# A static scheduler with other durations, VectorE/GpSimd access in its plan, paced attention, and two thirds of batch 0 masked by multiplication

## The chip, the cores and the metric

The kernel runs on one core of a Trainium2 chip, in one launch. The metric is the device time of one execution in microseconds (us). Five engines work beside each other, each through its own queue in order: TensorE (PE in the profile: matmuls; its weight loads are PEld), VectorE (DVE), ScalarE (ACT), GpSimd (POOL) and SyncE (SP, which only issues transfers here).

## The reference

Block-sparse attention (4 batches, 8 heads, 768 positions, head width 64), then a two-layer network with a squared relu on the 3072 x 512 result.

```python
scores = scale * np.matmul(q, k.transpose(0, 1, 3, 2))
mask = np.abs(blk_i - blk_j) <= window          # blocks of 32, window 1
mask = mask | (blk_i == 0) | (blk_j == 0) | (blk_i == n_blocks - 1) | (blk_j == n_blocks - 1)
for qb in range(n_blocks):
    for kb in sampled_blocks[qb]:               # 3 drawn blocks per query block
        mask[qb * block:(qb + 1) * block, kb * block:(kb + 1) * block] = True
scores = np.where(mask, scores, -1000000000.0)
attn = softmax(scores)
x = matmul(attn, v) as 3072 x 512
out = (np.maximum(x @ w_in, 0.0) ** 2) @ w_out  # 512 -> 2048 -> 512
```

## The kernel before

**Pairs and slots.** Two heads of one batch form a pair, 16 in all, 0 to 3 being batch 0. Work on attention is cut into 144 slots, each of one pair, 256 query columns (`qi`, 0 to 2) and 256 keys (`cp`, 0 to 2). Batch 0 goes by query third, then pair, then keys: slots 0 to 11 are `qi` 0 of its four pairs. From slot 36 on a pair's nine slots follow each other.

**A slot.** `scores` (L323) makes eight groups of 64-row matmuls, two heads side by side, into one of two PSUM buffers `ps`. `exps` (L341) is one exponential of 128 x 1024 on ScalarE into `pT`. `values` (L355) multiplies `pT` by the values, eight 65-wide matmuls into `po`; the 65th column gives the row sum. After three slots `normalize` (VectorE), `x_transp` (TensorE) and `x_evac` write 256 columns of `xT`.

**The mask** comes in two ways. In batch 0 `scores` adds it: four more matmuls on L337 of the block mask `R2` by `oh`. In the other batches `masks` (L346) multiplies `pT` on VectorE by `MK`, a 0/1 mask in SBUF that `mask_tile` and `mask_evac` (L258, L265) make in six tiles of 768 columns.

**Making a pair ready** (`prepare`, L459). For batch 0 queries and keys are cast to bfloat16 (`cast_qk`), transposed on TensorE (`transp`) and copied out (`evac`, into `QK`); from pair 4 on a DMA transposes (`transp_dma`, on SP's queue). Loads of pairs 4 and on wait at `loads_gate` until named parts of the network's weights have landed. `w_load` (L304) issues the weights in eight parts on GpSimd's queue, after the values of pair 2 were cast.

**Dense part.** `hidden`, `relu`, `square`, `output`, `out_copy`, `store`, over tiles of 256 tokens (batch 0) and 384 tokens. A relu goes to VectorE or ScalarE, a square to GpSimd, ScalarE or VectorE.

**Who orders all this.** Each step is a `Task` with engines and durations in us (`T_({"DVE": 0.57, "POOL": 1.0}, key, ...)`), the tasks it depends on, buffers it takes and gives back. `run_schedule` (L96) runs a plan when the program is built: of all ready tasks it takes the one with the earliest start, then the smallest key, puts it on the engine that would end first (plus a `bias`), and emits its instructions. Its durations set only the order in each engine's queue; at run time the engines wait on semaphores alone.

Of the kernel before, what the change touches and what calls it, by code (L numbers as in the profile page):

```python
# [25 lines left out]
def kernel(  # L26
# [32 lines left out]
    NRAW, NPB = 4, 6  # L59
# [17 lines left out]
    LAT = {"PE": 0.2, "DVE": 0.08, "ACT": 0.08, "POOL": 0.08, "SP": 2.0}  # L77
    SWITCH = 0.15
# [5 lines left out]
    class Task:  # L84
        def __init__(self, engs, key, fn, deps=(), get=(), put=(), after=0.0, mode=None, dma=0.0, late=None, bias={}):
# [3 lines left out]
            self.after, self.mode, self.dma, self.late, self.bias = after, mode, dma, late, bias  # L89
            self.end = self.eng = None  # L90
            self.order = len(tasks)
            for b in self.put:
                b.holds += 1
            tasks.append(self)

    def run_schedule(free, bufs, dma_free, mode=128):  # L96
        taken = {name: [] for name in bufs}
        waiting = list(tasks)
# [6 lines left out]
        while waiting or ready:  # L105
# [5 lines left out]
            best = None  # L111
            for t in ready:
# [26 lines left out]
            t.end = free[e] = end  # L139
# [42 lines left out]
    load(3, (sc_, sy, sc_))  # L182
# [39 lines left out]
    sbf = consts.tile([nb, n_rand], F32, name="sbf")  # L222
    edge = consts.tile([nb, 2], F32, name="edge")
    pm = consts.tile([nb, 4, nb], F32, name="pm")
    V.tensor_scalar(out=pm[:, 0, :], in0=rel, scalar1=-1.0, scalar2=None, op0=AOP.is_ge)
    V.scalar_tensor_tensor(out=pm[:, 1, :], in0=rel, scalar=1.0, in1=pm[:, 0, :],
                           op0=AOP.is_le, op1=AOP.mult)
    V.tensor_scalar(out=edge[:, 0:1], in0=row, scalar1=0.0, scalar2=None, op0=AOP.is_equal)
    V.tensor_scalar(out=edge[:, 1:2], in0=row, scalar1=float(nb - 1), scalar2=None, op0=AOP.is_equal)
    V.tensor_scalar(out=pm[:, 0, :], in0=pm[:, 1, :], scalar1=edge[:, 0:1], scalar2=edge[:, 1:2],  # L230
                    op0=AOP.max, op1=AOP.max)
    V.memset(pm[:, 0, 0:1], 1.0)
    V.memset(pm[:, 0, nb - 1:nb], 1.0)
    V.tensor_copy(out=oh[D:P, :], in_=oh[0:D, :])
    V.tensor_copy(out=sbf, in_=sb_i.rearrange("q (r two) -> q r two", two=2)[:, :, 0])
    cur = 0
    for r in range(n_rand):
        V.scalar_tensor_tensor(out=pm[:, 1 - cur, :], in0=col, scalar=sbf[:, r:r + 1],
                               in1=pm[:, cur, :], op0=AOP.is_equal, op1=AOP.max)
        cur = 1 - cur  # L240
    for c0 in (0, D):
        V.tensor_scalar(out=bm[:, c0:c0 + nb], in0=pm[:, cur, :], scalar1=-1.0, scalar2=-NEG,
                        op0=AOP.add, op1=AOP.mult)
# [5 lines left out]
    pb = ps_s.tile([P, 1024], F32, name="pb", tag="ps")  # L249
    for j, c0 in enumerate((0, 512)):  # L250
        w = min(512, S - c0)
        nc.tensor.matmul(pb[:, c0:c0 + w], bm, oh[0:nb, c0:c0 + w], start=True, stop=True)
    A.copy(out=R2[:, 0:QW], in_=pb[:, 0:QW])
    A.copy(out=R2[:, QW:S], in_=pb[:, QW:S])
# [3 lines left out]
    def mask_tile(n, e):  # L258
        pk = ps_s.tile([P, 1024], F32, name="pk", tag="ps")
        for c0 in (0, 512):  # L260
            w = min(512, S - c0)
            nc.tensor.matmul(pk[:, c0:c0 + w], oh[:, n * P:(n + 1) * P], R2[:, c0:c0 + w], start=True, stop=True)
        mtile[n] = pk

    def mask_evac(n, e):  # L265
        pk = mtile.pop(n)
        if e == "ACT":
            A.activation(out=MK[:, n, :], in_=pk[:, 0:S], func=AF.Exp)  # L268
        else:
            V.tensor_scalar(out=MK[:, n, :], in0=pk[:, 0:S], scalar1=-1.0, scalar2=None, op0=AOP.is_ge)  # L270
# [13 lines left out]
    def transp(u, w, e):  # L284
        src = cast.pop((u, w))
        pt = ps_h.tile([P, S], BF, name="pt", tag="h")
        for n in range(NCH):
            nc.tensor.transpose(pt[:, n * P:(n + 1) * P], src[:, n].rearrange("p t d -> p (t d)"), identb)
        ttile[u, w] = pt

    def evac(u, w, e):
        copy(e, QK[u % NPB][:, w, :], ttile.pop((u, w)))

    def transp_dma(u, w, e):
        sy.dma_start(out=QK[u % NPB][:, w, :].rearrange("r (n p) -> r n p", p=P),
                     in_=cast.pop((u, w)).rearrange("p n t d -> p (n t d)"), transpose=True)

    w_in_sb = consts.tile([P, KM, d_ff], BF, name="w_in_sb")
# [5 lines left out]
    def w_load(i, e):  # L304
        if i < NWP:
# [143 lines left out]
    def arrive(u, w):  # L449
        return 5.7 + 1.6 * (3 * u + w)  # L450
# [8 lines left out]
    def prepare(u):  # L459
        s0 = first[u]  # L460
        tr[u], ev[u] = [], []
# [3 lines left out]
        if u >= HP:  # L465
            g = gate[2] if u == HP else gate[5] if u == HP + 1 else gate[7]
            ld_t = T_(("SP", 1.0), s0 - 30, load, u, (sy, sy, sy),
                      deps=cv[u - NRAW] + tr[u - NRAW] + [g], dma=4.3)
            at = dict(deps=[ld_t])
            for w in (1, 0):  # L470
                qc = Buf("qc")
                c = T_({"DVE": 0.57, "POOL": 1.0}, s0 - 12, cast_qk, u, w, get=[qc], **at)
                tr[u].append(c)
                ev[u].append(T_(("SP", 1.0), s0 - 10, transp_dma, u, w, deps=[c] + old_s, put=[qc], dma=1.2))
        else:
            at = dict(after=arrive(u, 2))
            for w in (0, 1):
                qc, hb = Buf("qc"), Buf("h")
                opts = {"ACT": 0.75} if u == 0 and w else {"DVE": 0.57}
                c = T_(opts, s0 - 6, cast_qk, u, w, after=arrive(u, w), get=[qc])  # L480
                tr[u].append(c)
                t = T_(("PE", 0.36), s0 - 5, transp, u, w, deps=[c], get=[hb], put=[qc], mode=128)
                ev[u].append(T_({"DVE": 0.57} if w else {"ACT": 0.75, "DVE": 0.57}, s0 - 4, evac, u, w, deps=[t], put=[hb]))
        cv[u] = [T_({"POOL": 1.0} if u in (1, 2) else {"POOL": 1.0, "DVE": 0.57}, s0 - 2, cast_v, u,
                    deps=at.get("deps", []) + old_v, after=at.get("after", 0.0))]
# [6 lines left out]
    def attend(group, add):  # L492
        s = min(order.index(a) for a in group)
        bufs = {a: Buf("ps") for a in group}
        u0 = [a[0] for a in group]
        sc = T_(("PE", (0.44 if add else 0.22) * len(group)), s, scores, group, add,
                deps=sum((ev[u] for u in u0), []) + sc_all[-1:], get=[bufs[a] for a in group], mode=64)
        sc_all.append(sc)
        for a in group:
# [9 lines left out]
            va = T_(("PE", 0.40), s + 2.2, values, a, deps=[ex] + cv[u] + va_all[-1:],  # L509
# [3 lines left out]
            if cp == CP - 1:  # L513
                b, a_ = divmod(u, HP)
                nm = T_(("DVE", 0.55), s - 9, normalize, u, qi, deps=[va])
# [5 lines left out]
                mu[u, qi] = T_({"DVE": 0.25, "ACT": 0.36}, s - 9, x_evac, u, qi, deps=[xt], put=[ob[u, qi]], **kw)  # L521

    sc_all, va_all, ob = [], [], {}
    for u in range(NU):
        sc_of[u], va_of[u] = [], []
    for us in [range(HP)] + [[u] for u in range(HP, NU)]:
# [17 lines left out]
    RELU = {256: {"DVE": 0.35, "ACT": 0.42}, 384: {"DVE": 0.48, "ACT": 0.50}}  # L544
    SQ = {256: {"POOL": 0.65, "ACT": 0.42, "DVE": 0.35}, 384: {"POOL": 0.82, "ACT": 0.50, "DVE": 0.48}}
    sq_of, n_key = {}, 1000.0
    gbuf, hbuf = {}, {}
    for k_, T in enumerate(TILES + [None]):
# [4 lines left out]
        for _, kind, x in sorted(both, key=lambda z: z[:2]):  # L553
# [3 lines left out]
            if kind == 0:  # L557
# [11 lines left out]
                sq_of[x] = T_(SQ[w], n_key, square, t, f, deps=[rr], get=[gb], put=[rb], bias={"ACT": 1.5, "DVE": 1.5})  # L569
            else:  # L570
# [47 lines left out]
```

## Time and profile before

| what | value |
|---|---|
| median of three runs | 309.04 us (308.96 to 312.02) |
| the profiled execution: time, span | 309.11 us, 307.4 us |
| TensorE, VectorE, ScalarE, GpSimd busy | 93%, 66%, 56%, 50% of the span |
| exponentials (L343) | 144, mean 1026 ns, from 12.58 us to 224.5 us |
| mask multiplications (L350) | 108, mean 822 ns |
| mask matmuls in batch 0 (L337) | 144 |
| squares on GpSimd (L421) | 144 |
| relus on VectorE, on ScalarE (L412, L410) | 112, 32 |

Rows of the view by stage give a stretch in us, its length, then per engine the busy time and the number of instructions in it, at the end the granted share of TensorE's clock, the share of the DMA engines and GB/s. Rows by form give line, engine, operation, output and inputs, shapes, count, busy us and mean ns, then the engine's idle time before these and who ended it. Timeline rows begin with start and duration in us.

### The profile page before, as it was taken

To read this page: it belongs to the slowest core of one execution; us is meant where nothing else is said; L and a number is where in the kernel's file an instruction comes from. 1 tells how busy PE (TensorE), PEld (TensorE's weight loads), DVE (VectorE), ACT (ScalarE), POOL (GpSimd) and SP (SyncE) were. 2 spreads that over 40 slices of the span, in tenths; PEclk is the share of its full clock that TensorE was granted. 3 is DMA by queue.
4 is the path that set the end of the run, shared out by engine and by line. 5 is a ranking of instruction groups with operands and counts; after the bars stand their busy time and mean duration, and the time that the engine had idled before them with its cause. 6 is when DMAs were issued, how large, how long until landed. Compare 5 with 4: busy or idle time off the path is not lost.

```text
span 307.4 us, 7318 instructions
## 1 busy us (share of the span) xinstructions
PE 284.8 (93%) x3002; PEld 166.2 (54%) x3002; DVE 203.1 (66%) x411; ACT 172.0 (56%) x217; POOL 152.6 (50%) x187
## 2 busy tenths in 40 slices
PE   6798999899898989889989999999989999999994
PEld 2456766675655544555546556455545555555542
DVE  7573334989998887889987787878774444444410
ACT  1878989107777877777878779788721000000011
POOL 4280111798756560466673344244436665666620
PEclk9999999999999999999999999999999999999999
DMA  7999998697999981320200000000100111000012
GB/s 259 355 138 205 260 256 304 175 280 205 255 232 247 256 199 48 74 53 2 51 2 36 3 34 2 36 35 2 36 0 36 41 50 49 35 34 36 34 47 89
DMA packets 40011, 34.55 MB, mean 112 GB/s; under 512 B 20522, under 2 KB 36906, under 8 KB 39978
## 3 DMA queue, kind: packets, MB, share of 16 engines
q1 hardware_dynamic: 34122, 27.53, 31.2%
q0 software_dynamic: 4224, 4.19, 8.5%
q10 hardware_dynamic: 1632, 2.36, 2.2%
q8 instruction: 23, 0.38, 0.5%
q14 instruction: 10, 0.08, 0.1%
HBM read 27.26 MB, written 6.29 MB: 109 GB/s over the span
## 4 chain that ended last, share of the span: by engine, by line
PE 59%; DVE 19%; ACT 10%; issue 5%; DMA 3%; POOL 2%; SPq 0%; ACTq 0%; DVEq 0%; POOLq 0%
PE ph L403 21%; PE py L433 20%; DVE pT L350 10%; PE po L366 7%; ACT pT L343 7%; PE ps L333 7%; DVE r L412 3%; DVE qc L158 2%; DVE xq L375 2%; POOL g L421 2%; DMA qs<-in_q_dram 2%; PE po L382 2%; PE ps L337 2%; DMA vs<-in_v_dram 1%; ACT MK L268 1%
## 5 line engine op out<-in xcount | busy, mean ns | idle before, releaser
L421 POOL TENSOR_TENSOR g<-r 128x384 bf16<-128x384 f32 (+1 forms) x144 | 125.0, 877 | 119.4 <-DVE r L412 96.0
L343 ACT ACTIVATE pT<-ps 128x1024 bf16<-128x1024 f32 x144 | 140.0, 1026 | 36.9 <-PE ps L333 32.4
L403 PE MATMUL ph<-xT,w_in_sb 128*128 128x384 bf16 (+1 forms) x576 | 108.7, 309 | 0.4 <-DVE r L412 0.3
L433 PE MATMUL py<-w_out_sb,g 128*128 128x512 bf16 x384 | 104.2, 379 | 0.1
L350 DVE TENSOR_TENSOR pT<-pT,MK 128x1024 bf16<-128x1024 bf16 x108 | 87.2, 822 | 6.5 <-ACT pT L343 6.4
L412 DVE TENSOR_SCALAR r<-ph 128x384 f32<-128x384 f32 (+1 forms) x112 | 57.1, 513 | 42.1 <-POOL g L421 24.0
L403 PEld LDWEIGHTS <-w_in_sb 128*128 128x128 bf16 x576 | 51.1, 98 | 36.7 <-issue 6.9
L366 PE MATMUL po<-VT,pT 128*128 128x65 bf16 x1152 | 54.0, 194 | 8.2 <-DVE pT L350 6.3
L366 PEld LDWEIGHTS <-pT 128*128 128x128 bf16 x1152 | 44.1, 98 | 30.5 <-DVE pT L350 15.4
L156 ACT COPY ys<-py 128x512 f32<-128x512 f32 x21 | 12.3, 587 | 77.2 <-PE py L433 77.1
L333 PE MATMUL ps<-QK 64*128 64x256 bf16 x576 | 52.1, 272 | 1.8 <-ACT pT L343 0.8
L433 PEld LDWEIGHTS <-g 128*128 128x128 bf16 x384 | 35.3, 98 | 25.9 <-issue 2.1
L333 PEld LDWEIGHTS <-QK 64*128 64x128 bf16 x576 | 24.2, 94 | 18.4 <-issue 11.6
L373 DVE RECIPROCAL rs<-po 128x4 f32<-128x4 f32 x48 | 8.6, 179 | 29.8 <-PE po L366 29.7
L375 DVE TENSOR_TENSOR xq<-po,rs 128x256 bf16<-128x256 f32 x48 | 20.4, 424 | 1.7
L410 ACT ACTIVATE r<-ph 128x384 f32<-128x384 f32 (+1 forms) x32 | 14.5, 454 | 8.0 <-PE ph L403 7.5
L337 PE MATMUL ps<-R,oh 64*128 64x256 bf16 x144 | 17.7, 269 | 0.0
L382 PE MATMUL po<-identb,xq 128*128 128x128 bf16 x96 | 13.5, 222 | 3.9 <-DVE xq L375 3.6
L158 POOL CAST VT<-vs 128x768 bf16<-128x768 f32 x8 | 7.0, 883 | 20.1 <-PE po L366 12.1
L382 PEld LDWEIGHTS <-xq 128*128 128x128 bf16 x96 | 6.7, 97 | 16.0 <-DVE xq L375 11.6
L158 DVE COPY xT<-po 128x256 bf16<-128x256 bf16 x36 | 10.2, 284 | 2.5 <-PE po L382 2.5
L158 DVE CAST qc<-qs 128x768 bf16<-128x768 f32 x11 | 7.7, 700 | 0.0
(50 smaller groups left out, 83.7 us busy)
## 6 DMA issues: line engine op xcount, KB each, us to landing
out_dram<-ys SPq DMA_DIRECT2D x24, 256.0 KB, 2.0
qs<-in_q_dram SPq DMA_DIRECT2D x14, 384.0 KB, 4.7
vs<-in_v_dram SPq DMA_DIRECT2D x14, 384.0 KB, 6.5
ks<-in_k_dram SPq DMA_DIRECT2D x14, 384.0 KB, 4.9
w_in_sb<-in_moe_w_in_dram POOLq DMA_DIRECT2D x4, 512.0 KB, 7.9
w_out_sb<-in_moe_w_out_dram POOLq DMA_DIRECT2D x4, 512.0 KB, 19.9
ks<-in_k_dram ACTq DMA_DIRECT2D x2, 384.0 KB, 6.0
qs<-in_q_dram ACTq DMA_DIRECT2D x2, 384.0 KB, 5.2
```

The lines of the kernel that those rows point to most:

```text
L158: (V if e == "DVE" else G).tensor_copy(out=out, in_=in_)
L333: nc.tensor.matmul(ps[:, h, c, :], QK[i][hs, 1, ksl], QK[i][hs, 0, qsl], start=c == 0, stop=not add, skip_group_check=True)
L337: nc.tensor.matmul(ps[:, h, c, :], oh[hs, ksl], R2[hs, qsl], start=False, stop=True, skip_group_check=True)
L343: A.activation(out=pT, in_=stile.pop(a), func=AF.Exp, scale=scale)
L350: V.tensor_tensor(out=pT, in0=pT, in1=m[:, None].broadcast_to([P, 2, 2, QW]), op=AOP.mult)
L366: nc.tensor.matmul(po[:, qc, h, :], pT[:, h, c, qc * P:(qc + 1) * P], VT[i][:, h, n, 0:VW], start=(n == 0 and qc == 0 and h == 0), stop=n ...
L375: V.tensor_tensor(out=xq, in0=po[:, :, :, 0:D], in1=rs.broadcast_to([P, 2, 2, D]), op=AOP.mult)
L382: nc.tensor.transpose(pt[:, qc * P:(qc + 1) * P], xq[:, qc].rearrange("p h d -> p (h d)"), identb)
L403: nc.tensor.matmul(ph, w_in_sb[:, kc, f * P:(f + 1) * P], xT[b][:, kc, c0:c0 + w], start=(kc == 0), stop=(kc == KM - 1))
L412: V.tensor_scalar(out=r, in0=src, scalar1=0.0, scalar2=None, op0=AOP.max)
L421: (G if e == "POOL" else V).tensor_mul(out=g, in0=r, in1=r)
L433: nc.tensor.matmul(py, gtile[T, f][:, ts * P:(ts + 1) * P], w_out_sb[:, f, :], start=(f == 0), stop=(f == NF - 1))
```

## The change

The scheduler's tables get other durations and latencies, with a part of each task (`OVER`) that overlaps the next one on its engine. Tasks marked `port` are lengthened in the plan where VectorE and GpSimd work at once. Tasks with keys from 100 up may not be put ahead of an urgent one on their engine (`AHEAD`). Scores from slot 36 on are planned no earlier than 40 + 1.7 us per slot. In batch 0 only slots 0 to 11 add the mask by matmul; slots 12 to 35 go in twos and are multiplied on VectorE. The mask tiles are cut into 512 and 256 columns, in the buffers `h`. Pair 0 is cast, transposed and copied in two parts. A load of values moves from ScalarE's queue to SP's; the weight loads move ahead, behind a small copy (`held`) that waits for the keys of pair 2. Squares may no longer go to VectorE, and go to ScalarE with a smaller bias. The mask's preparation on small tiles is written with fewer instructions, and the copy of `oh` moves to ScalarE.

```diff
-    NRAW, NPB = 4, 6
+    NRAW, NPB, QC_BUFS = 4, 6, 5
...
-    LAT = {"PE": 0.2, "DVE": 0.08, "ACT": 0.08, "POOL": 0.08, "SP": 2.0}
-    SWITCH = 0.15
+    LAT = {"PE": 0.23, "DVE": 0.06, "ACT": 0.06, "POOL": 0.08, "SP": 2.0}
+    OVER = {"PE": 0.0, "DVE": 0.08, "ACT": 0.09, "POOL": 0.03, "SP": 0.0}
+    SWITCH = 0.1
+    AHEAD = {"PE": 0.05, "DVE": 0.2, "ACT": 0.25, "POOL": 0.0, "SP": 0.0}
+    LEAD = 12.0
+    PACE0, PACE, SINGLE, MASK_AT = 40.0, 1.7, 1, 12.0
...
+                    if e == "POOL" or (e == "DVE" and t.port):
+                        p0, p1 = port["DVE" if e == "POOL" else "POOL"]
+                        us += 0.7 * max(0.0, min(r + us, p1) - max(r, p0))
...
+            best = min((c for c in found if c[1] < 100 or c[0] + AHEAD[c[4][2]] < urgent.get(c[4][2], 1e9)),
+                       key=lambda c: c[:3], default=None)
...
-            t.end = free[e] = end
+            t.end, free[e] = end, end - OVER[e]
...
-    load(3, (sc_, sy, sc_))
+    load(3, (sc_, sy, sy))
...
-    V.tensor_copy(out=oh[D:P, :], in_=oh[0:D, :])
+    A.copy(out=oh[D:P, :], in_=oh[0:D, :])
...
     def w_load(i, e):
+        if i == 0:
+            G.tensor_copy(out=held, in_=raw[2][1][0:1, 0, 0, 0:2])
...
-                c = T_({"DVE": 0.57, "POOL": 1.0}, s0 - 12, cast_qk, u, w, get=[qc], **at)
+                c = T_({"DVE": 0.55, "POOL": 1.2}, 101, cast_qk, u, w, slice(0, NCH), bias={"POOL": 0.5}, get=[qc], port=True,
+                       after=PACE0 + PACE * (s0 - HP * NQ * CP) - LEAD, **at)
...
+            for ns in (slice(0, 2), slice(2, NCH)) if u == 0 else (slice(0, NCH),):
...
-                wl[i] = T_(("POOL", 1.2), s0 - 3 + i, w_load, i, deps=cv[HP - 2], late=2.0, dma=3.6)
+                wl[i] = T_(("POOL", 0.85), -50 + i, w_load, i, after=12.6, late=2.2, dma=2.65)
...
         sc = T_(("PE", (0.44 if add else 0.22) * len(group)), s, scores, group, add,
-                deps=sum((ev[u] for u in u0), []) + sc_all[-1:], get=[bufs[a] for a in group], mode=64)
+                deps=[ev[u][w, 2 if n else 0] for u, qi, cp in group for w, n in ((0, qi), (1, cp))]
+                + (mr[:1 + (group[0][1] > 0)] if add else []) + sc_all[-1:], get=[bufs[a] for a in group], mode=64,
+                after=PACE0 + PACE * (s - HP * NQ * CP) if s >= HP * NQ * CP else 0.0)
...
-            ex = T_(("ACT", 0.95), s, exps, a, deps=[sc], get=[pt], put=[bufs[a]])
+            ex = T_(("ACT", 1.02), s, exps, a, deps=[sc], get=[pt], put=[bufs[a]])
             if not add:
-                ex = T_(("DVE", 0.6), s - 1, masks, a, deps=[ex, mk[cp * 2], mk[cp * 2 + 1]])
+                ex = T_(("DVE", 0.68), s - 1, masks, a, deps=[ex, mk[cp * 2, qi], mk[cp * 2 + 1, qi]], port=True)
...
-            for a in mine:
+            singles = [a for a in mine if a[1] < SINGLE]
+            for a in singles:
                 attend([a], True)
+            mine = [a for a in mine if a not in singles]
+            for i in range(0, len(mine) - 1, 2):
+                attend(mine[i:i + 2], False)
...
-    RELU = {256: {"DVE": 0.35, "ACT": 0.42}, 384: {"DVE": 0.48, "ACT": 0.50}}
-    SQ = {256: {"POOL": 0.65, "ACT": 0.42, "DVE": 0.35}, 384: {"POOL": 0.82, "ACT": 0.50, "DVE": 0.48}}
+    RELU = {256: {"DVE": 0.424, "ACT": 0.39}, 384: {"DVE": 0.557, "ACT": 0.49}}
+    SQ = {256: {"POOL": 0.613, "ACT": 0.39}, 384: {"POOL": 0.826, "ACT": 0.49}}
...
-                sq_of[x] = T_(SQ[w], n_key, square, t, f, deps=[rr], get=[gb], put=[rb], bias={"ACT": 1.5, "DVE": 1.5})
+                sq_of[x] = T_(SQ[w], n_key, square, t, f, deps=[rr], get=[gb], put=[rb], bias={"ACT": 0.5})
```

What the tables do shows in the queues. First ScalarE at the start, from its loads on; before:

```order
L173 DMA ks<-in_k_dram 128x2x384
L173 DMA qs<-in_q_dram 128x2x384
L173 DMA vs<-in_v_dram 128x2x384
L184 ACT_TABLE_LOAD
L253 CAST R_175<-pb 128x256
L254 CAST R_175<-pb 128x512
L156 CAST qc<-ks 128x768
L268 ACTIVATE MK<-pk 128x768 x2
L343 ACTIVATE pT<-ps 128x1024 x3
```

and now:

```order
L187 DMA ks<-in_k_dram 128x2x384
L187 DMA qs<-in_q_dram 128x2x384
L198 ACT_TABLE_LOAD
L248 COPY oh<-oh 64x768
L170 CAST qc<-ks 128x256
L170 CAST R_172<-pb 128x256
L170 CAST qc<-ks 128x512
L359 ACTIVATE pT<-ps 128x1024 x3
L281 ACTIVATE MK<-pk 128x512
```

A load of values (`vs`) and two mask tiles are gone from ahead of the first exponential, and the keys (`qc<-ks`) stand in two parts around the first part of the mask rows.

Then VectorE in batch 0, behind the preparation of its last pair (`rs` and `xq` normalize, `r` is a relu); before, around the thirteenth slot:

```order
L373 RECIPROCAL rs<-po 128x4
L375 TENSOR_TENSOR xq<-po,rs 128x256
L158 COPY xT<-po 128x256
L412 TENSOR_SCALAR r<-ph 128x256
L373 RECIPROCAL rs<-po 128x4
```

and now:

```order
L389 RECIPROCAL rs<-po 128x4
L391 TENSOR_TENSOR xq<-po,rs 128x256
L366 TENSOR_TENSOR pT<-pT,MK 128x1024
L172 COPY xT<-po 128x256
L366 TENSOR_TENSOR pT<-pT,MK 128x1024
L283 TENSOR_SCALAR MK<-pk 128x256 x2
L366 TENSOR_TENSOR pT<-pT,MK 128x1024
```

Masks (`pT<-pT,MK`) and the evacuation of mask tiles (`MK<-pk`) stand between the steps of normalizing.

Last ScalarE in the later slots of batch 0 (`r` is a relu, `g` a square, `ys` an output copy). Before, all but the first six exponentials of batch 0 follow each other:

```order
L343 ACTIVATE pT<-ps 128x1024 x3
L268 ACTIVATE MK<-pk 128x768
L343 ACTIVATE pT<-ps 128x1024 x3
L268 ACTIVATE MK<-pk 128x768
L343 ACTIVATE pT<-ps 128x1024 x30
L410 ACTIVATE r<-ph 128x256 x3
L156 COPY ys<-py 128x512
```

now they go in twos with relus, squares and copies between:

```order
L435 ACTIVATE g<-r 128x256
L359 ACTIVATE pT<-ps 128x1024 x2
L426 ACTIVATE r<-ph 128x256 x2
L435 ACTIVATE g<-r 128x256
L359 ACTIVATE pT<-ps 128x1024 x2
L170 COPY xT<-po 128x256
L426 ACTIVATE r<-ph 128x256
L170 COPY ys<-py 128x512
```

So relus of batch 0 that stood on VectorE (35 of 48 tiles of 256 columns before, 8 now) and 28 squares of GpSimd are on ScalarE's queue.

More of the change, by code (lines that the diff above doesn't have):

```diff
@@ L97, in run_schedule @@
         taken = {name: [] for name in bufs}
+        port = {"DVE": (0.0, 0.0), "POOL": (0.0, 0.0)}
         waiting = list(tasks)
@@ L138, in run_schedule @@
             t.eng = e
-            t.end = free[e] = end
+            t.end, free[e] = end, end - OVER[e]
+            if e == "POOL" or (e == "DVE" and t.port):
+                port[e] = (at, end)
             if e == "PE" and t.mode:
@@ L248 @@
-    R2 = consts.tile([P, S], BF, name="R2")
[L249 to L254, printed above, removed]
-    MK = consts.tile([P, NCH, S], BF, name="MK")
-    def mask_tile(n, e):
-        pk = ps_s.tile([P, 1024], F32, name="pk", tag="ps")
+    V.memset(al[:, n_rand, 0:1], 1.0)
@@ L281, in cast_v, with transp @@
     def cast_v(u, e):
         copy(e, VT[u % NPB][:, :, :, 0:D], raw[u][2])
[L284 to L292, printed above, removed]
+    def transp(u, w, ns, e):
+        src = cast.pop((u, w, ns.start))
+        pt = ps_h.tile([P, NCH, P], BF, name="pt", tag="h")
+        for i, n in enumerate(range(ns.start, ns.stop)):
+            nc.tensor.transpose(pt[:, n], src[:, i].rearrange("p t d -> p (t d)"), identb)
+        ttile[u, w, ns.start] = pt
@@ L484, in prepare @@
-        cv[u] = [T_({"POOL": 1.0} if u in (1, 2) else {"POOL": 1.0, "DVE": 0.57}, s0 - 2, cast_v, u,
-                    deps=at.get("deps", []) + old_v, after=at.get("after", 0.0))]
+            at = dict(after=arrive[u][2])
+            for ns in (slice(0, 2), slice(2, NCH)) if u == 0 else (slice(0, NCH),):
+                n = ns.stop - ns.start
+                for w in (0, 1):
+                    qc, hb = Buf("qc"), Buf("h")
+                    opts = {"ACT": 0.23 + 0.1 * n} if u == 0 and w else {"DVE": 0.07 + 0.08 * n}
+                    if u:
+                        opts["POOL"] = 1.2
+                    c = T_(opts, s0 - 6 + ns.start, cast_qk, u, w, ns, after=arrive[u][w], get=[qc], port=True)
+                    tr[u].append(c)
+                    t = T_(("PE", 0.06 * n), s0 - 5 + ns.start, transp, u, w, ns, deps=[c], get=[hb], put=[qc], mode=128)
+                    opts = {"DVE": 0.14 + 0.07 * n}
+                    if u == 0:
+                        opts["ACT"] = 0.23 + 0.1 * n
+                    x = T_(opts, s0 - 4 + ns.start, evac, u, w, ns, deps=[t], put=[hb])
+                    for j in range(ns.start, ns.stop, 2):
+                        ev[u][w, j] = x
```

122 lines of the change are left out of this document (66 added, 56 removed).

## The prediction

> **What bounds the kernel now.** I read the page first (PE 93% busy), then busy time by stage, with the stage borders at the start of the exponentials (line L343) number 0, 12, 24, 36, 72, 108 and at the end of the last, then the matmuls by form.
>
> ```profile
> core 0 of [0], span 307.4 us
> core 0: us, PE busy (x) PEld busy (x) DVE busy (x) ACT busy (x) POOL busy (x), PEclk, DMA share, GB/s
> 0.00:12.58 12.58, 7.88 (x44) 3.46 (x46) 8.39 (x23) 4.39 (x6) 4.82 (x19) 1.00 0.86 303
> 12.58:28.10 15.52, 14.02 (x229) 9.77 (x229) 9.04 (x22) 12.73 (x15) 7.04 (x9) 1.00 1.03 195
> 28.10:40.70 12.60, 12.21 (x206) 8.65 (x203) 4.68 (x15) 11.54 (x14) 1.53 (x3) 1.00 1.18 237
> 40.70:70.10 29.40, 28.49 (x350) 19.80 (x348) 19.67 (x47) 13.38 (x16) 16.64 (x26) 1.00 0.84 249
> 70.10:122.90 52.80, 48.33 (x586) 28.57 (x582) 45.92 (x87) 40.58 (x53) 31.16 (x33) 1.00 0.84 210
> 122.90:175.90 53.00, 48.42 (x602) 28.35 (x598) 45.82 (x87) 40.95 (x52) 28.46 (x28) 1.00 0.14 32
> 175.90:224.50 48.60, 47.47 (x580) 27.20 (x577) 38.21 (x79) 40.34 (x51) 19.70 (x20) 1.00 0.06 23
> 224.50:303.20 78.70, 77.69 (x433) 40.36 (x431) 31.38 (x56) 7.54 (x14) 43.29 (x53) 1.00 0.11 41
> ```
>
> TensorE is never far from full, but its busy time stretches over waits: pipelined matmuls count from start to modelled end. So I price its work by the distance between starts where nothing waits.
>
> ```profile
> 240.00:300.00 60.00, 60.00 (x320) 1.00 0.10 39
> L433 PE MATMUL py<-w_out_sb,g 128*128 128x512 bf16 x156 | 40.5, 379 | 0.0
> L403 PE MATMUL ph<-xT,w_in_sb 128*128 128x384 bf16 x164 | 33.4, 326 | 0.0
> ...
> 12.04 0.29 PE L337 MATMUL ps<-R,oh 64*128 64x256 bf16 x2
> 12.15 0.29 PE L333 MATMUL ps<-QK 64*128 64x256 bf16 x2
> ...
> 172.50 0.42 PE L366 MATMUL po<-VT,pT 128*128 128x65 bf16 x8
> 172.75 0.49 PE L403 MATMUL ph<-xT,w_in_sb 128*128 128x384 bf16 x2
> ...
> 205.60 0.61 PE L333 MATMUL ps<-QK 64*128 64x256 bf16 x8
> 206.14 0.82 PE L403 MATMUL ph<-xT,w_in_sb 128*128 128x384 bf16 x4
> ```
>
> Dense stretch: 156 x 512 + 164 x 384 columns in 60.0 us are 0.42 ns per column, so 0.215 us for 512, 0.161 for 384, 0.108 for 256, 0.054 for 128. Two 64-row matmuls go together, 0.11 per pair (12.04 to 12.15). Eight 65-wide value matmuls take 0.25, about 0.03 each. Eight score matmuls (four pairs, 0.44) were followed only after 0.54: a change between 64-row and 128-row matmuls costs 0.10. All of the program:
>
> ```profile
> L433 PE MATMUL py<-w_out_sb,g 128*128 128x512 bf16 x384 | 104.2, 379 | 0.1
> L403 PE MATMUL ph<-xT,w_in_sb 128*128 128x384 bf16 x384 | 79.7, 326 | 0.0
> L366 PE MATMUL po<-VT,pT 128*128 128x65 bf16 x1152 | 54.0, 194 | 8.2 <-DVE pT L350 6.3 <-DVE xT L158 1.0 <-ACT pT L343 0.5
> L333 PE MATMUL ps<-QK 64*128 64x256 bf16 x576 | 52.1, 272 | 1.8 <-ACT pT L343 0.8 <-ACT MK L268 0.5
> L403 PE MATMUL ph<-xT,w_in_sb 128*128 128x256 bf16 x192 | 29.0, 273 | 0.4 <-DVE r L412 0.3
> L337 PE MATMUL ps<-R,oh 64*128 64x256 bf16 x144 | 17.7, 269 | 0.0
> L382 PE MATMUL po<-identb,xq 128*128 128x128 bf16 x96 | 13.5, 222 | 3.9 <-DVE xq L375 3.6
> ...
> 1.52 4.12 PE L199 MATMUL junk<-warm 128*128 128x512 bf16 x12 [1.52 <-DVE warm L191]
> ...
> 302.28 1.24 PE L433 MATMUL py<-w_out_sb,g 128*128 128x512 bf16 x5
> ```
>
> The sum: 82.6 + 61.9 + 34.6 + 31.7 (288 pairs) + 20.6 + 7.9 (72 pairs) + 5.2, and 9.0 for warm-up, the mask and the first transposes: 253.5. The order of the program has 184 changes of row mode: 18.4. Together 271.9 us of work between 1.5 and 303.1 us, so TensorE stands still for 301.6 - 271.9 = 29.7 us. That is what can be won beside work itself. Where it lies: from slot 72 to 107 (122.90 to 175.90) the order holds 44.9 us of work in 53.0, so 15% waiting, with VectorE 86% and ScalarE 77% busy. From slot 108 to 143 it holds 46.2 in 48.6, 5% waiting, with VectorE at 79%. After 224.5 next to nothing waits. So TensorE bounds the end; in the attention stages VectorE, with ScalarE close by, keeps it from its work.
>
> **Work removed.** In 24 of 36 slots of batch 0 the four mask matmuls on L337 go: 96 fall to 48 pairs of 0.11, 5.3 us. These slots go in twos, so the order has 164 row changes, 20 fewer: 2.0 us. TensorE's work becomes 264.6. If it waited nowhere, the end of this execution would be 1.5 + 264.6 + 4.3 (last matmul to span's end) + 1.7 (span to the 309.1 us of the profiled execution) = 272.1. That execution is within 0.1 us of the median of 309.04, so no conversion is needed.
>
> **Waits up to slot 12.** Today they are 28.1 - 1.5 - 18.7 = 7.9 us.
>
> ```profile
> 6.03 0.25 DVE L242 TENSOR_SCALAR bm<-pm 24x24 bf16<-24x24 f32 x2
> 6.20 0.54 DVE L158 CAST qc<-qs 128x768 bf16<-128x768 f32 x1
> ...
> 6.90 1.28 ACT L184 ACT_TABLE_LOAD   x1 [6.90 <-DMA qs<-in_q_dram]
> 8.94 0.84 ACT L156 CAST qc<-ks 128x768 bf16<-128x768 f32 x1
> 12.58 1.02 ACT L343 ACTIVATE pT<-ps 128x1024 bf16<-128x1024 f32 x1 [0.70 <-PE ps L337]
> ```
>
> ScalarE loads its table only behind its sixth load, so keys are cast at 8.94 though queries are cast at 6.20. With one load fewer on its queue the table is loaded early; then keys and queries go in parts. VectorE's row in front of the first score: 6.3 + 0.2 + 0.4 (two casts) + 0.5 (mask rows) + 2 x 0.28 (two part copies) = 8.0, scores 0.4: first exponential near 8.5, four us sooner. Bounds: none of it arrives (0), all four arrive. Pairs 1 to 3 still wait for the same input loads, and three mask tiles are on ScalarE here, so I take slot 12 at 23 us: 23 - 1.5 - 17.7 (work in the new order) = 3.8. The weight loads, now issued ahead of these pairs' last casts, I cost at nothing: the first use of them is after slot 22. If they came in the way, 1 to 2 us of late input at slot 9 would be next.
>
> **Slots 12 to 35.** Here work moves to ScalarE and VectorE.
>
> ```profile
> L343 ACT ACTIVATE pT<-ps 128x1024 bf16<-128x1024 f32 x144 | 140.0, 1026 | 36.9 <-PE ps L333 32.4 <-PE ps L337 3.9 <-PE ph L403 0.2
> L410 ACT ACTIVATE r<-ph 128x384 f32<-128x384 f32 x19 | 9.4, 497 | 0.9 <-PE ph L403 0.6
> L410 ACT ACTIVATE r<-ph 128x256 f32<-128x256 f32 x13 | 5.0, 390 | 7.0 <-PE ph L403 6.9
> ...
> L350 DVE TENSOR_TENSOR pT<-pT,MK 128x1024 bf16<-128x1024 bf16 x108 | 87.2, 822 | 6.5 <-ACT pT L343 6.4
> ...
> L350 DVE TENSOR_TENSOR pT<-pT,MK x108: 674/691/1344, 71.2 to 225.3; 128x1024 bf16<-128x1024 bf16 x108
> ```
>
> ScalarE has 24 exponentials, 16 relus, 4 squares and 5 small ones: 24 x 1.03 + 20 x 0.39 + 2.5 = 35.0, less 0.05 each for overlap (140.0 us busy over 144 against a mean of 1.026) = 32.4. A square on ScalarE is not in the trace; I take it as a relu of its size, between the half and the double (0.2 to 0.8; 28 of them, so -5 to +11 us of ScalarE time, mostly beside other work). VectorE gets 24 masks, 24 x 0.82 = 19.7; with its normalizing, casts and mask tiles it has about 32, as much as ScalarE. TensorE has 27.8 in the new order. So this stage takes 32.4 and TensorE waits 4.6; slot 36 starts at 55 instead of 70, with dense work that stood alone between 55 and 70 done beside it or left for later.
>
> By the Trainium skill's page "SBUF — State Buffer" (section "Who interferes with whom") a VectorE instruction with two SBUF inputs and a GpSimd instruction that reads SBUF exclude each other for a whole instruction. The trace agrees: masks run from 674 to 1344 ns. By that rule moving masks into a stage in which GpSimd squares is the risky part of this change; it makes the fourth case below.
>
> **The way to slot 36.** Keys and queries of pair 4 come through SP's queue, where their transposes stand, in both orders, behind gated loads.
>
> ```profile
> 48.12 0.42 SPq L173 DMA_DIRECT2D vs<-in_v_dram  x1
> 54.61 2.64 SPq L295 DMA_TRANSPOSE QK<-qc  x2
> ```
>
> Those loads were through at 48.5, and the two transposes took 2.64 to issue. Needed at 70 today, they are now needed at 55, with pair 4's casts on VectorE among the masks of the last batch 0 slots, at 48 to 53 by my times. So slot 36 can be up to 2 us late with everything behind it on TensorE's queue; I leave that inside the 9% below.
>
> **Slots 36 to 143.** The dense work is spread: the new order has 86.9 us of TensorE work in slots 36 to 98 and 75.5 in 99 to 143, 56.7 behind the last scores instead of 78.5. VectorE's relus fall from 112 to 66, GpSimd's squares from 144 to 116, both given to ScalarE (32 to 78 relus, 28 squares). In slots 36 to 98 ScalarE has 63 exponentials, 47 relus, 10 squares and 8 small ones: 93.6, or 86.7 less the overlap, equal to TensorE's 86.9; VectorE has some 68 at its undisturbed times. Today's slots 108 to 143 (TensorE 46.2, ScalarE 44 with its overlap not yet taken off) wait 5%, slots 72 to 107 with a fuller VectorE 15%. A stage with ScalarE as full as TensorE and VectorE freer lies between; I take 9%, 86.9 / 0.91 - 86.9 = 8.6. In slots 99 to 143 TensorE's 75.5 stand over ScalarE's 65.7 and VectorE's 61, a wider lead than in any stage today; 3.5%, 2.7 us. Bounds: 5% and 15% over all 162.4 give 8.5 and 28.7, and two or three less than 8.5 if TensorE's lead covers all.
>
> **The sum.** 272.1 + 3.8 + 4.6 + 8.6 + 2.7 = 291.8, forecast **292 us**, 17 less than now: 7.3 from work, 10 from waits.
>
> **Rivals.** *The waits stay*: only the work goes, 309.1 - 7.3 = 302. For it: an order by other durations still fixes each engine's queue, and every late operand holds all behind it. Against: the start and the VectorE load both ease. *TensorE hardly waits*: 3 + 2 + 3.5% of 162.4 give 272.1 + 10.7 = 283. For it: today's last attention stage; against: ScalarE's new load.
>
> *Slower: ScalarE's loop.* Scores have two PSUM buffers. A pair's scores can be followed only when its exponentials are through, and each time ScalarE then waits for TensorE: today 32.4 us, in the trace 37 times, 0.88 each. If its relus and squares don't fill this gap, each pair of slots pays 0.88 on ScalarE: 12 pairs in slots 12 to 35 give +10.6; slots 36 to 98 become 86.7 + 31.5 x 0.88 = 114.4 instead of 95.5, +18.9; slots 99 to 143 61 + 22.5 x 0.88 = 81 instead of 78, +2.7. That is 292 + 32 = 324. From 0.6 us per pair on it eats the whole gain. For it: the row of waits. Against: between 28.10 and 40.70 ScalarE was busy 11.54 of 12.60, 0.18 per two slots, and 0.46 per two slots between 175.90 and 224.50, with few fillers.
>
> *Masks meet squares*: a mask that loses takes 1.34 instead of 0.82; 16 squares stand in slots 12 to 35, so at most 16 x 0.52 = 8.3 on a VectorE that has no slack there: 300.
>
> **Chances.** Forecast 0.60, waits stay 0.17, hardly waits 0.12, masks meet squares 0.05, ScalarE's loop 0.06. A run can tell a change of 1% from none, 306 to 312 us. The loop case falls into it when it is partly filled (0.02), and the waits-stay case when TensorE's waits also grow by 4 (0.03). So faster 0.91, same 0.05, slower 0.04. The range holds the forecast with both wait bounds (281 to 305 less their tails): 283 to 303.
>
> **What would show it.** First exponential near 8.5 us, the thirteenth near 23, the thirty-seventh near 55, the last near 230; 48 matmuls on the mask line; masks nearer 691 than 822 ns on the mean; dense work alone for some 57 us behind the last scores; ScalarE's waits for scores no longer than today's 32.4 us. The forecast is wrong if the attention stages have more than 15% of waiting by the same rates, or if slot 36 starts after 62 us.

## The result

| kernel | median | runs |
|---|---|---|
| before | 309.65 us | 308.96 to 312.02, 4 runs |
| changed | 287.27 us | 287.12 to 287.60, 4 runs |

The ratio is 0.927 (95% interval 0.921 to 0.932): 22 us, 7.3% faster. The profiled execution of the changed kernel took 287.3 us, its span is 285.4. The forecast was 292, with 283 to 303 as its range.

Busy time by stage in the profile after, with the borders at the starts of exponentials 0, 12, 36 and 99, at the end of the last, and at the last matmul:

```profile
core 0: us, PE busy (x) PEld busy (x) DVE busy (x) ACT busy (x) POOL busy (x), PEclk, DMA share, GB/s
0.00:8.70 8.70, 6.15 (x34) 2.59 (x34) 6.37 (x21) 3.41 (x5) 3.36 (x18) 1.00 0.80 279
8.70:24.34 15.64, 13.84 (x212) 8.99 (x213) 11.47 (x24) 13.48 (x16) 9.00 (x12) 1.00 1.17 272
24.34:59.36 35.02, 32.38 (x426) 21.26 (x425) 29.89 (x60) 31.33 (x52) 17.91 (x22) 1.00 1.11 268
59.36:149.91 90.55, 88.77 (x1116) 53.53 (x1113) 71.23 (x137) 84.24 (x129) 48.02 (x52) 1.00 0.48 136
149.91:225.56 75.65, 75.54 (x822) 42.62 (x821) 58.37 (x116) 60.14 (x84) 21.39 (x23) 1.00 0.20 46
225.56:281.20 55.64, 55.64 (x303) 28.73 (x300) 20.45 (x38) 5.77 (x10) 30.21 (x36) 1.00 0.12 43
```

In the long attention stages (slots 36 to 98 and 99 to 143) TensorE is now busy 88.77 of 90.55 and 75.54 of 75.65 us. VectorE is busy 79% and 77% of them; before, it was busy 87%, 86% and 79% of the three stages between 70.10 and 224.50 us. By the prediction's rates (work in the order against elapsed time) the waits are: up to slot 12 24.3 - 1.5 - 17.7 = 5.1 us, slots 12 to 35 35.0 - 27.8 = 7.2, slots 36 to 98 90.6 - 86.9 = 3.7, slots 99 to 143 75.6 - 75.5 = 0.1. Behind the last scores 56.7 us of work took 55.6, so the borders of stages are good to a microsecond or two: counted by the matmuls that start inside each stretch, the waits from slot 12 on are 5.0, 3.3 and 0.8 us. The total does not hang on borders. Up to the start of the last matmul at 281.1 us TensorE stands still for 281.1 - 1.5 - 264.6 = 15.0 us, 29.7 before. So 7.3 us came from less work and 14.7 from waits. The mask matmuls are 48, as the order had said, and ScalarE waits for scores 11.9 us instead of 32.4:

```profile
L353 PE MATMUL ps<-R,oh 64*128 64x256 bf16 x48 | 5.9, 269 | 0.0
...
ACT pT L359 <- PE ps L349: 11.9, 25, 1.8
```

The start, on ScalarE's timeline: the table is loaded at 3.43 instead of 6.90, the first part of the keys cast at 5.58 instead of 8.94.

```profile
3.43 1.28 ACT L198 ACT_TABLE_LOAD   x1 [3.43 <-issue]
4.72 0.83 ACT L248 COPY oh<-oh 64x768 bf16<-64x768 bf16 x1
5.58 0.41 ACT L170 CAST qc<-ks 128x256 bf16<-128x256 f32 x1
6.17 0.37 ACT L170 CAST R<-pb 128x256 bf16<-128x256 f32 x1 [0.18 <-PE pb L266]
6.43 0.62 ACT L170 CAST qc<-ks 128x512 bf16<-128x512 f32 x1
8.70 1.02 ACT L359 ACTIVATE pT<-ps 128x1024 bf16<-128x1024 f32 x1 [1.65 <-PE ps L353]
```

### The profile page after: what moved, and what is told of

It is laid out like the page before. It is cut to its first block, busy times and chain, and to the rows that moved or that the text cites. A ratio compares the mean times of both kernels' runs of the same rounds, so it can differ in the third digit from the quotient of the medians.

```text
span 285.4 us, 7135 instructions
## 1 busy us (share of the span) xinstructions
PE 272.6 (96%) x2906; PEld 157.7 (55%) x2906; DVE 197.8 (69%) x392; ACT 199.0 (70%) x294; POOL 129.9 (46%) x161
## 4 chain that ended last, share of the span: by engine, by line
PE 79%; DVE 14%; ACT 3%; issue 2%; ACTq 0%; DVEq 0%
PE py L449 27%; PE ph L419 25%; PE po L382 12%; PE ps L349 11%; DVE pT L366 7%; DVE qc L172 2%; ACT pT L359 2%; PE po L398 2%; PE junk L213 1%; DVE xq L391 1%; DVE xT L172 1%; PE pt L301 1%; DVE rs L389 1%; DVE QK L172 1%; DVE r L428 0%
## 5 line engine op out<-in xcount | busy, mean ns | idle before, releaser
L437 POOL TENSOR_TENSOR g<-r 128x384 bf16<-128x384 f32 (+1 forms) x116 | 101.9, 885 | 133.0 <-ACT r L426 70.5
L359 ACT ACTIVATE pT<-ps 128x1024 bf16<-128x1024 f32 x144 | 140.0, 1024 | 15.4 <-PE ps L349 11.9
L366 DVE TENSOR_TENSOR pT<-pT,MK 128x1024 bf16<-128x1024 bf16 x132 | 101.5, 781 | 11.3 <-ACT pT L359 11.2
L419 PE MATMUL ph<-xT,w_in_sb 128*128 128x384 bf16 (+1 forms) x576 | 106.4, 308 | 0.0
L428 DVE TENSOR_SCALAR r<-ph 128x384 f32<-128x384 f32 (+1 forms) x66 | 35.5, 538 | 29.8 <-POOL g L437 15.3
L349 PE MATMUL ps<-QK 64*128 64x256 bf16 x576 | 47.5, 272 | 1.1 <-ACT pT L359 0.8
L349 PEld LDWEIGHTS <-QK 64*128 64x128 bf16 x576 | 22.4, 94 | 27.7 <-issue 23.1
L426 ACT ACTIVATE r<-ph 128x256 f32<-128x256 f32 (+1 forms) x78 | 31.9, 446 | 4.2 <-PE ph L419 3.8
L435 ACT ACTIVATE g<-r 128x384 bf16<-128x384 f32 (+1 forms) x28 | 13.4, 478 | 5.8 <-DVE r L428 5.4
L172 POOL CAST VT<-vs 128x768 bf16<-128x768 f32 x15 | 14.1, 939 | 6.1 <-DMA vs<-in_v_dram 5.4
L398 PEld LDWEIGHTS <-xq 128*128 128x128 bf16 x96 | 7.3, 97 | 11.4 <-DVE xq L391 5.8
L172 DVE COPY xT<-po 128x256 bf16<-128x256 bf16 x36 | 10.2, 285 | 1.5 <-PE po L398 1.4
L172 DVE CAST qc<-ks 128x768 bf16<-128x768 f32 x14 | 11.1, 790 | 0.0
```

What stands on the lines that cost most here:

```text
L172: (V if e == "DVE" else G).tensor_copy(out=out, in_=in_)
L349: nc.tensor.matmul(ps[:, h, c, :], QK[i][hs, 1, ksl], QK[i][hs, 0, qsl], start=c == 0, stop=not add, skip_group_check=True)
L359: A.activation(out=pT, in_=stile.pop(a), func=AF.Exp, scale=scale)
L366: V.tensor_tensor(out=pT, in0=pT, in1=m[:, None].broadcast_to([P, 2, 2, QW]), op=AOP.mult)
L398: nc.tensor.transpose(pt[:, qc * P:(qc + 1) * P], xq[:, qc].rearrange("p h d -> p (h d)"), identb)
L419: nc.tensor.matmul(ph, w_in_sb[:, kc, f * P:(f + 1) * P], xT[b][:, kc, c0:c0 + w], start=(kc == 0), stop=(kc == KM - 1))
```

## The experiments

Where did the 14.7 us of waits go, and does the work count in full? Twelve kernels take one thing or a group of things back from the change, or add it to the kernel before. All medians are beside runs of the kernel before on the same chip, whose medians were 309.0 to 310.0 us.

| kernel | median us | ratio to before, 95% |
|---|---|---|
| change, all masks by matmul | 290.4 | 0.935 to 0.941 |
| change, old table for relu and square | 288.0 | 0.928 to 0.933 |
| change, no pacing | 288.7 | 0.930 to 0.935 |
| change, value matmuls planned at 0.40 | 292.4 | 0.940 to 0.948 |
| change, all old durations, no shared access | 302.8 | 0.974 to 0.984 |
| change, urgent tasks not protected | 290.4 | 0.939 to 0.942 |
| change, old start | 288.4 | 0.930 to 0.938 |
| change, no shared access in the plan | 294.0 | 0.950 to 0.954 |
| before, masks as changed | 309.5 | 0.995 to 1.002 |
| before, value matmuls planned at 0.245 | 311.9 | 1.005 to 1.011 |
| before, all new durations | 307.9 | 0.994 to 1.000 |
| before, durations, protection and masks | 309.3 | 0.999 to 1.004 |

The change itself has 0.921 to 0.932. The intervals of the old table, of no pacing and of the old start overlap this, so their 0.7 to 1.4 us are hints only. One thing more blurs the profiles by up to 1.4 us: with the same instructions at the start, the first exponential came at 8.70 to 8.94 us in three of them, the change among them, and at 9.57 to 10.08 us in five (masks by matmul, value matmuls at 0.40, no pacing, no protection, no shared access). In the three TensorE's twelve warm-up matmuls took 4.2 to 4.8 us, in the five 5.0 to 5.3, and the mask rows stood behind them.

**Does the removed work count?** The masks taken back alone:

```diff
-    PACE0, PACE, SINGLE, MASK_AT = 40.0, 1.7, 1, 12.0
+    PACE0, PACE, SINGLE, MASK_AT = 40.0, 1.7, 3, 12.0
```

> The changed kernel, but all 36 slots of batch 0 add their mask by matmul, as before the change (SINGLE = 3). TensorE's work rises by 7.3 us to 271.9, VectorE loses 24 masks. Theory A (work counts in full, since TensorE bounds the end): 287.3 + 7.3 = 294.6, between 293 and 296. Rival B (in slots 12 to 35 ScalarE is the bound and TensorE has 7.2 us of waits, which swallow the mask matmuls): 287 to 290.

It came between the two: 3.1 us slower than the change, not 7.3. By the same rates its waits are 284.8 - 1.5 - 271.9 = 11.4 us, 3.6 less than in the change. Masks moved to VectorE free TensorE of 7.3 us and give half of it back as waits. They come back in slots 12 to 35: here, without these masks on VectorE, the matmuls that start in this stage, mask matmuls included, are 31.5 us of work in 32.3, in the change 30.0 in 35.0. And the other way, the masks alone on the kernel before:

```diff
-            for a in mine:
-                attend([a], True)
             for n in range(NCH):
...
-                t = T_(("PE", 0.33), 24 + 2 * n, mask_tile, n, get=[mb], mode=128)
+                t = T_(("PE", 0.33), 2 + 2 * n, mask_tile, n, get=[mb], mode=128)
...
+            singles = [a for a in mine if a[1] < 1]
+            for a in singles:
+                attend([a], True)
+            mine = [a for a in mine if a not in singles]
+            for i in range(0, len(mine) - 1, 2):
+                attend(mine[i:i + 2], False)
```

> The kernel before with one part of the change alone: slots 12 to 35 go in twos and are multiplied on VectorE, the mask tiles are made ahead of them; the old durations, the old start. TensorE's work falls by 7.3 us. Theory A (work counts, waits are another matter): 309.5 - 7.3 = 302, between 300 and 304. Rival B (24 more masks on a full VectorE and mask tiles ahead of the first slots eat it): 307 to 312. Rival C (the twos also let the plan start dense work earlier, so that waits fall too): below 299.

309.5 us: the time of rival B, though the run does not show that VectorE and the mask tiles are what eats the gain. Part of it is TensorE's clock (last section): its runs at full clock took 307.1 to 307.6, against 308.6 to 309.3 of the kernel before at full clock. So of 7.3 us of work less than 2 reach the end there.

**Is it relus and squares off VectorE and GpSimd?** My reason for slots 36 on.

```diff
-    RELU = {256: {"DVE": 0.424, "ACT": 0.39}, 384: {"DVE": 0.557, "ACT": 0.49}}
+    RELU = {256: {"DVE": 0.35, "ACT": 0.42}, 384: {"DVE": 0.48, "ACT": 0.50}}
...
-sq_of[x] = T_(SQ[w], n_key, square, t, f, deps=[rr], get=[gb], put=[rb], bias={"ACT": 0.5})
+sq_of[x] = T_(SQ[w], n_key, square, t, f, deps=[rr], get=[gb], put=[rb], bias={"ACT": 1.5, "DVE": 1.5})
```

> The changed kernel with the durations and biases of relus and squares of before, which puts 79 relus on VectorE (66 in the change) and 143 squares on GpSimd (116). Theory A (the waits from slot 72 on went because VectorE lost relus and met fewer squares of GpSimd): 5 to 7 us slower, 292 to 295. Rival B (they went because the plan as a whole fits the chip, whichever engine has the relus): within 2 us, 286 to 289.

288.0: only 0.7 us, so this reason carries little. It is not a full test: of the 46 relus that VectorE lost 13 came back, and 27 of GpSimd's 28 squares. **Or that the plan knows of shared access?**

```diff
-                        us += 0.7 * max(0.0, min(r + us, p1) - max(r, p0))
+                        us += 0.0 * max(0.0, min(r + us, p1) - max(r, p0))
```

> The changed kernel whose plan no longer lengthens what VectorE and GpSimd do at the same time; relus on VectorE rise from 66 to 86, squares on ScalarE fall from 28 to 14. Theory A (the plan needs to know of shared access): masks above 0.80 us on the mean (0.78 in the change) and 1 to 4 us slower, 288 to 291. Rival B (TensorE's lead covers it): 286.5 to 288.

294.0, 6.7 us slower, more than either theory gave. The masks and squares of the kernel with the old table, of this one, then of the change:

```profile
L366 DVE TENSOR_TENSOR pT<-pT,MK 128x1024 bf16<-128x1024 bf16 x132 | 107.4, 831 | 5.3 <-ACT pT L359 5.2
L437 POOL TENSOR_TENSOR g<-r 128x384 bf16<-128x384 f32 (+1 forms) x143 | 131.7, 931 | 107.6 <-DVE r L428 65.0 <-ACT r L426 42.4
```

```profile
L366 DVE TENSOR_TENSOR pT<-pT,MK 128x1024 bf16<-128x1024 bf16 x132 | 104.7, 804 | 5.9 <-ACT pT L359 5.5
L437 POOL TENSOR_TENSOR g<-r 128x384 bf16<-128x384 f32 (+1 forms) x130 | 118.1, 916 | 126.0 <-DVE r L428 81.6 <-ACT r L426 41.1 <-DVE rs L389 1.7
```

```profile
L366 DVE TENSOR_TENSOR pT<-pT,MK 128x1024 bf16<-128x1024 bf16 x132 | 101.5, 781 | 11.3 <-ACT pT L359 11.2
L437 POOL TENSOR_TENSOR g<-r 128x384 bf16<-128x384 f32 (+1 forms) x116 | 101.9, 885 | 133.0 <-ACT r L426 70.5 <-DVE r L428 56.7 <-DVE rs L389 5.7
```

The first of them, with the old table, has the most collisions (masks 831 ns on the mean, 143 squares at 931) and loses 0.7 us. The second, whose plan is blind to them, has fewer (804 and 916) and loses 6.7. So the number of collisions does not decide. That the order reckons with them fits all three kernels; but the blind plan also puts 86 relus on VectorE (79 with the old table), and no run separates the two. Most of the loss shows in slots 99 to 143: 81.3 us for 76.0 of work, where the change needs 75.6 for 75.5. Of the rest, 2.0 us stood ahead of slot 36, half of it ahead of the first exponential.

```profile
152.70:234.00 81.30, 77.57 (x829) 42.99 (x826) 66.30 (x121) 53.59 (x68) 35.84 (x35) 1.00 0.17 43
```

In its waits TensorE's value matmuls stand for masks three times as long as in the change, and with the old table, for all its collisions, no longer than there. Here are the blind plan, the change and the old table:

```profile
PE po L382 <- DVE pT L366: 5.5, 14, 1.2
```

```profile
PE po L382 <- DVE pT L366: 1.7, 5, 0.7
```

```profile
PE po L382 <- DVE pT L366: 1.3, 5, 0.3
```

**The other durations.** One of them, which made TensorE look fuller than it is:

```diff
-            va = T_(("PE", 0.245), s + 2.2, values, a, deps=[ex] + cv[u] + va_all[-1:],
+            va = T_(("PE", 0.40), s + 2.2, values, a, deps=[ex] + cv[u] + va_all[-1:],
```

> The changed kernel with one duration of before: 0.40 us for a slot's value matmuls instead of 0.245. The plan then takes TensorE for fuller than it is, and the order has 64.0 us of work in slots 99 to 143 (75.5 in the change) and 76.8 behind them (56.7). Theory A (durations that fit let the plan lay dense work into TensorE's gaps; this is where the waits went): 5 to 9 us slower, 292 to 296. Rival B (the gain is that of the start and of the masks, the durations are a detail): 287 to 289.

292.4, 5.1 us slower, as theory A had it: with 64.0 instead of 75.5 us of work in slots 99 to 143, 76.8 stand behind them and earlier gaps stay unfilled (waits 20.2 us). All durations of before, with `OVER` at 0 and no shared access (the edit in part; `LAT`, `SWITCH`, the durations of values, normalizing and copies and the tables of relu and square went back too):

```diff
-    OVER = {"PE": 0.0, "DVE": 0.08, "ACT": 0.09, "POOL": 0.03, "SP": 0.0}
+    OVER = {"PE": 0.0, "DVE": 0.0, "ACT": 0.0, "POOL": 0.0, "SP": 0.0}
...
-            ex = T_(("ACT", 1.02), s, exps, a, deps=[sc], get=[pt], put=[bufs[a]])
+            ex = T_(("ACT", 0.95), s, exps, a, deps=[sc], get=[pt], put=[bufs[a]])
...
-                ex = T_(("DVE", 0.68), s - 1, masks, a, deps=[ex, mk[cp * 2, qi], mk[cp * 2 + 1, qi]], port=True)
+                ex = T_(("DVE", 0.6), s - 1, masks, a, deps=[ex, mk[cp * 2, qi], mk[cp * 2 + 1, qi]], port=True)
```

> The changed kernel with all durations, latencies and overlaps of before and no shared access in the plan; masks, start, pacing and weight loads as changed. Theory A: work down by 7.5 us, waits as before but for the start, 299 to 305. Rival B: 287 to 291.

302.8, with waits of 30.3 us (296.2 - 1.5 - 264.4): as many as before. In the new structure the plan's numbers, its reckoning with shared access among them, are worth 15.5 us, all the waits that went. Yet in the old structure the same numbers bring next to nothing:

> The kernel before with this one duration of the change: 0.245 us for a slot's value matmuls. Its order has 61.6 us in slots 99 to 143 (57.9 before) and 70.7 behind them (78.4). Theory A: a third to a half of the gain in waits, 302 to 305. Rival B: 308 to 311.

Edit: `0.40` to `0.245` in `values`' task. 311.9, slower by 0.5 to 1.1%: no theory had a slower one. TensorE's clock fell here too, for 6.8 us.

> The kernel before with all durations, latencies and overlaps of the change, but its own masks, start, pacing and no shared access in the plan. TensorE's work stays at 272 us. Theory A (the durations take the waits away): 295 to 301. Rival B (waits go by the start and by the masks): 307 to 311.

Edit: all of these numbers the other way round, in the kernel before. 307.9, in rival B's range, but the run does not show B's reason.

**What makes the numbers pay?** Candidates were the protection of urgent tasks, pacing and the start.

```diff
-            best = min((c for c in found if c[1] < 100 or c[0] + AHEAD[c[4][2]] < urgent.get(c[4][2], 1e9)),
+            best = min((c for c in found if True or c[0] + AHEAD[c[4][2]] < urgent.get(c[4][2], 1e9)),
```

> The changed kernel without the rule that a task with a key from 100 up must not delay an urgent one on its engine. Theory A (durations work only with this rule, which keeps relus, squares and casts from standing ahead of exponentials and masks): 4 to 8 us slower, 291 to 295. Rival B (durations alone order the queues well): 287 to 289.

290.4, 3.1 us: less than A, more than B.

```diff
-    PACE0, PACE, SINGLE, MASK_AT = 40.0, 1.7, 1, 12.0
+    PACE0, PACE, SINGLE, MASK_AT = 0.0, 0.0, 1, 12.0
```

> The changed kernel without the earliest start times of scores and casts (PACE0 = PACE = 0). The order then has 64.8 us of TensorE work in slots 99 to 143 instead of 75.5 and 68.9 behind them instead of 56.7. Theory A (spreading dense work evenly keeps TensorE fed): waits in slots 99 to 143 rise from nothing to some 5%, 3 to 4 us, 290 to 292. Rival B (pacing changes the order but TensorE bounds all of it anyway): 287 to 288.

288.7, 1.4 us: nearer to B. Slots 99 to 143 took 64.6 us for 64.8 of work, so theory A's waits did not come. Of the waits that came back 1.2 us stand ahead of the first exponential, behind the longer warm-up, where pacing moved nothing.

```diff
-    load(3, (sc_, sy, sy))
+    load(3, (sc_, sy, sc_))
...
-            for ns in (slice(0, 2), slice(2, NCH)) if u == 0 else (slice(0, NCH),):
+            for ns in (slice(0, NCH),):
```

(and the weight loads and the copy of `oh` as before)

> The changed kernel with the start of before: pair 0 in one part, six loads on ScalarE's queue, the copy of oh on VectorE, weight loads behind the values of pair 2. The first exponential comes again near 12 us (8.7 in the change). Theory A (TensorE bounds the rest, so a later start is paid in full): 3 to 4 us slower, 290 to 291.5. Rival B (slots 12 to 35 hang on ScalarE and on weights, which hide it): 287 to 288.5.

288.4, 1.1 us, rival B. Slot 12 started 3.9 us later than in the change, slot 36 3.0, slot 99 1.5: the later stages took it up. Part of the 3.9 is not the start itself: in this profile TensorE's granted clock was a half from 9.4 to 16.2 us. Last, masks, durations and protection together on the kernel before:

> The kernel before with the durations of the change, its rule on urgent tasks and its masks in batch 0; old start, old weight loads, whole mask tiles, no pacing, no shared access in the plan. TensorE's work is 264.6 us, as in the change. Theory A (these three are the gain, the start is worth some 3 us): 290 to 295. Rival B (what is left out, loads, casts and mask tiles, makes the durations pay): 298 to 304.

309.3, slower than either theory. TensorE's work is that of the change, and still nothing is won. Its stages between 100 and 140 us:

```profile
100.00:110.00 10.00, 8.14 (x119) 4.69 (x118) 8.93 (x19) 7.57 (x10) 2.05 (x2) 1.00 0.93 261
110.00:120.00 10.00, 6.65 (x82) 4.03 (x82) 8.67 (x16) 6.19 (x8) 4.37 (x4) 0.69 1.09 281
120.00:130.00 10.00, 8.97 (x81) 5.36 (x80) 5.79 (x13) 6.28 (x7) 1.07 (x2) 0.50 0.21 39
130.00:140.00 10.00, 8.78 (x103) 5.04 (x102) 9.45 (x14) 7.30 (x12) 8.80 (x8) 0.96 0.01 2
```

Here VectorE is busy 8.9 of 10 with TensorE at 8.1 and then 6.7, while loads fill the DMA engines (0.93, 1.09); then the granted clock falls to 0.50, and a matmul of 384 columns takes 320 ns from start to start instead of 162. The chain of waits runs through VectorE in this stretch, with a cast of keys or queries (`qc`) between the masks:

```profile
102.62 0.40 DVE pT L354
103.02 0.37 issue
103.38 1.17 DVE qc L162
104.56 0.60 DVE pT L354
105.16 0.60 DVE ys L162
105.76 1.20 DVE pT L354 x2
...
113.90 0.71 DVE qc L162
114.61 0.20 DVE xT L162
114.81 3.49 DVE pT L354 x3
```

In the change the DMA share over slots 36 to 98 is 0.48: its casts have an earliest time and a late key, so pairs are made ready shortly before their slots. The last load of values, on SP's timeline of this kernel and then of the change (in the kernel before it stands at 106.16):

```profile
113.87 0.47 SPq L177 DMA_DIRECT2D vs<-in_v_dram  x1
```

```profile
141.71 0.47 SPq L187 DMA_DIRECT2D vs<-in_v_dram  x1
```

That casts and loads so early spoil the plan is argued from these rows, not shown: no run moved the casts alone. It also stays open how the 22 us between this kernel and the change divide among the casts' places, the shared access (6.7 us in the new structure), the start (1.1), pacing (1.4), the finer mask tiles and the clock (half of it for 17.1 us, at most 8.5 us).

None of the twelve has a lower median than the changed kernel.

## Why the prediction was right, and where its reasons were not

- **What bounds.** Right: TensorE's work by start distances, 271.9 and 264.6 us, plus waits makes both times, and its waits were the larger thing to win. The rates count four score matmuls to a slot (576 in 144 slots), which is what the kernel has; the description of a slot says eight.
- **Work removed, 7.3 us.** Right as a term of TensorE's sum. As a gain it was not independent of the waits: taken back it costs 3.1 us, and alone on the kernel before it brings under 2.
- **Up to slot 12.** First exponential forecast near 8.5, measured 8.70; slot 12 at 23, measured 24.34; waits 3.8, measured 5.1. The earlier loads, table and casts came as forecast, but 8.70 is in part luck: where the warm-up took longer, the same start gave up to 10.08, and I had no such wait. Its worth at the end was about 1.1 us: I had counted a later start in full.
- **Slots 12 to 35.** 32.4 forecast, 35.0 measured, so slot 36 started at 59.4 and not near 55. That 35.0 is also the sum of ScalarE's rows before I took off the overlap is chance: ScalarE was busy 31.3 of it and VectorE 29.9. I read this as two nearly full engines that wait for each other. With all masks by matmul both were emptier (24.2 and 17.2 us) and the stage took 32.3, filled by TensorE; no run took only one of them away.
- **Slots 36 to 143.** The mis-sized term: 8.6 + 2.7 us of waits forecast, 3.7 + 0.1 measured. ScalarE was busy 93% of slots 36 to 98, about as I had reckoned (91%), but did not hold TensorE up.
- **The reason for it** did not bear out: I had hung these waits on how full VectorE and ScalarE are, but 13 relus and 27 squares given back cost 0.7 us, and the plan's numbers taken back, with the rest of the change kept, cost 15.5. I had costed the shared access only as longer masks and not as an order that goes wrong. My sign for it, masks nearer 691 than 822 ns on the mean, failed too: 781.
- **Rivals.** ScalarE's loop did not come: it waited 11.9 us for scores. *Masks meet squares* did not decide. *The waits stay* is what the change was with the old durations: 302.8 against 302 forecast.

The errors, +1.3 and +2.6 us before slot 36, -4.9 and -2.6 after it and about -1.1 behind the last scores, add up to the 4.7 us by which the forecast was too high.

## What to carry to other kernels

A static order is as good as its durations: here they were worth 15.5 us, where the operations taken off the busiest engine were worth 3.1. Give the plan what two engines cost each other when they meet: here an order that reckoned with collisions bore more of them than one that did not. And measure such a thing in the structure where it will be used: on the kernel before, the same numbers brought next to nothing. Why, stays open; inputs made ready too early are the suspect.

## What the runs showed of the hardware

TensorE's granted clock fell to a half in the middle of a run, with TensorE still at work, ahead of the last scores in five of the fourteen profiles: with durations, protection and masks together on the kernel before for 17.1 us from 113.8, with the new durations there for 10.2 us from 119.7, with its masks as changed for 10.2 us from 116.4, with its value matmuls at 0.245 for 6.8 us from 119.3, and in the change with the old start for 6.8 us from 9.4.

Waits alone do not bring this about: the kernel before waited 15% of slots 72 to 107, the change with the old durations 30.3 us in all, and both kept 1.00 in their profiles up to the last matmul. Cut each profile into pieces of 3.41 us from the moment at which its record of the granted clock begins (4.3 to 7.3 us); every fall and return in the fourteen lies on such a border. With the prediction's rates, row changes left out, TensorE's work fills 33 to 38% of the piece just ahead of each of the five falls. No piece at full clock that was followed by another at full clock holds less than 40%. The two sides are close, and no run was made to look for the border between them.

So an order that leaves TensorE this short for some 3.4 us pays twice: for the wait, and then for slower matmuls. That the longest single wait in the 10 us ahead of the falls was 1.9 us shows that it does not take one long stop.
